# Another hand-written order for batch 0 of a hash-masked attention followed by a gated MLP

## The chip, the cores and the metric

The kernel runs on one core of one Trainium2 chip. The time is that of the device, in microseconds, from one launch of the whole program; the median of several runs counts. The profile is of one execution, whose own time is given beside the span of its instructions.

## The reference

Attention over 4 batches, 8 heads, 768 positions and 64 numbers per head. A query sees a key only if the signs of six projections of both agree. What it gives is put together into 3072 tokens of 512 numbers, which pass a GEGLU layer with a gated residual.

```python
q_bits = (np.einsum('bhsd,dk->bhsk', q, proj) > 0)
k_bits = (np.einsum('bhsd,dk->bhsk', k, proj) > 0)
mask = q_bucket[:, :, :, None] == k_bucket[:, :, None, :]
scores = np.where(mask, scale * np.matmul(q, k.transpose(0, 1, 3, 2)), -1e9)
attn = softmax(scores)
x = np.matmul(attn, v).transpose(0, 2, 1, 3).reshape(B * S, H * D)
g = x @ w_gate
ffn_out = (0.5 * g * (1 + erf(g / sqrt(2))) * (x @ w_val)) @ w_out
out = x + ffn_out / (1 + exp(-(x @ w_res)))
```

## The kernel before

**Tiling.** Two heads make a pair, four pairs a batch, so there are 16 pairs, numbered 0 to 15; pairs 0 to 3 are batch 0. Side 0 of a pair is q, side 1 is k. Positions are laid out as 128 partitions by 6 tiles for each head. An operand tile `aug` has 64 rows of data and 7 rows of hash bits, so that one product gives the score and the mask together.

**Making an operand.** `load` brings q or k into `ld` (four buffers for each side), `load_v` brings v into `ldv` (three buffers). `tr` transposes 32x32 blocks on VectorE into `t32`; `hash_mm` multiplies these with the projection on TensorE in fp32 (jobs h00 to h33, four pieces for each group of pairs in `HASHES`); `hash_tok` turns the sums back (tk); `bits` writes the signs beside the data in one of four `nat` tiles (bt). `cast` writes the data there in bf16 on GpSimd (cs). A `nat` tile is shared by a pair's side and the same side of the pair two further on. The operand is then turned either on TensorE, six tile transposes by `turn_pe` (tp, with pair, side and head in its name) and a copy out of PSUM by `turned` (td), or by one DMA transpose on SyncE's queue, `turn` (tu). For q and k of pairs 1 to 3 the first way is taken, for pairs 4 to 7 the second. `bits` of a k side in batch 0 has two of its four writes on GpSimd and two on VectorE.

**Values.** `vals_a` casts v to bf16 with a column of ones (va), `vals_s` sums v (vs), both on GpSimd.

**A score piece.** Each pair has nine pieces; batch 0 has s0 to s35. `scores` writes 1024 columns of PSUM from TensorE (two buffers, `sc_ps`) and ScalarE's exp (L553) empties them into a ring of nine places. `values` (v0 to v35) multiplies eight blocks of it with v. `finish` (fin) divides by the sum; for pairs 0 and 1 of batch 0 a DMA transpose turns the result, for pairs 2 and 3 TensorE does (`x_turn`, jobs xt2 and xt3).

**The order.** The scheduling is manual: each engine runs its instructions in the order in which the program issues them, and waits where an operand is not ready. What stands ahead of the list is fixed: the first loads (those of pair 0, then `FIRST_LOADS` in its order, all on SyncE's queue), the hashes of pair 0's first head, and on GpSimd in this order the cast of pair 1's q, `vals_a(0)`, the cast of pair 1's k, the copies that make `projw` (needed by every h job) and `vals_s(0)`. Then the jobs of `ORDER` are issued one after the other, s0 to s35 among them, ending with g0 and g1 (the first three of four products of the gate and the value of block 0), xt3 and three hash pieces. Jobs ho and hoq are the fp32 hashes of pair 0's second head, bo0 and bo1 their bits.

After it `gate_val(0)` runs twelve blocks m of the hidden layer: gate product, value product (both L566), gelu on ScalarE (L583), product on VectorE (L586). `BESIDE[m]` lists the jobs that are issued behind block m. Batches 1 to 3 run in loops: score pieces with the output products (L598, L614) of the batch before between them, then their own `gate_val`.

**Weights.** `load_w` issues the next of twelve weight loads on GpSimd's queue, whichever w job is met: w0 to w7 are gate and value by turns in quarters of three blocks each, w8 is the residual gate's matrix, w9 to w11 the output matrix in thirds.

Of the kernel before, what the change touches and what calls it, by code (L numbers as in the profile page):

```python
# [13 lines left out]
PSUM = bass.MemoryType.PSUM  # L14


FIRST_LOADS = [(1, "q"), (0, "v"), (1, "k"), (2, "q"), (2, "k"), (2, "v"), (3, "q"), (3, "k"), (1, "v")]
HASHES = [(0, (1,)), (1, (2, 3)), (2, (4, 5)), (3, (6, 7))]
X_PE = 2
ORDER = """  # L20
trq tpB tdk tdq trk s0 hoq tr10 ld50 s1 bo0 s2 ho bo1 tp001 td001 s3 tp011 td011a ld40 tr11 ld51 v0
v1 cs21 td011b s4 s5 h00 h01 h02 h03 tr20 s6 s7 v2 v3 v4 tk0 bt10 bt11 tp100 tp110 td100 td110 tr21
s8 tr30 tr31 tp111 td111 cs31 s9 tp101 td101 s10 w0 v5 v6 v7 v8 s11 cs20 s12 ld61 fin00 ld41 h10 h11
w1 s13 h12 h13 fin01 cs30 s14 lv3 ld70 s15 va1 v9 v10 v11 s16 tk1 bt20 bt21 bt31 tp200 tp210 td200
td210 vs1 s17 tp211 td211 cs41 tr50 s18 tp201 td201 va2 s19 tp310 vs2 s20 vs3 bt30 td310 v12 v13 s21
v14 fin10 s22 tp300 tr40 w2 tp301 s23 v15 tr51 s24 lv4 va4 v16 v17 s25 v18 s26 v19 v20 v21 td301
td300 s27 fin11 v22 s28 cs50 tp311 s29 ld71 v23 fin20 w3 w4 s30 lv5 w5 v24 v25 td311 s31 v26 fin21
va3 tr41 v27 s32 w6 v28 v29 v30 s33 xt2 s34 v31 s35 gelu tr61 v32 v33 v34 g0 v35 fin30 op40 g1 fin31
xt3 ld60 h20 h21 h22 w7
"""  # L30
BESIDE = [
    "vs4 lv6 cs40 h23 tk2 bt41",
    "cs51 bt50",
    "tu50 cs70 tr70",
    "bt40 tu40 cs60 w8 w9 w10 w11",
    "bt51",
    "tr71",
    "tu51",
    "tr60",
    "h30 h31 h32 tu41 cs61 h33 tk3 bt60 bt61 tu60 tu61",  # L40
    "cs71 bt71 tu71",
    "bt70 tu70",
    "pr40 rp40",
]

@with_exitstack
def kernel(
# [57 lines left out]
    def load(p, side, eng=None):  # L105
        b, hp = divmod(p, HP)
        s = ld_pool.tile([P, HT, D], FP32, tag=f"ld{side}", name=f"ld{side}")
        (eng or nc.sync).dma_start(
            s.rearrange("p (h t) d -> p h (t d)", h=2),
            (q, k)[side][b, 2 * hp:2 * hp + 2].rearrange("h (p t) d -> p h (t d)", t=T))  # L110
        raw[p, side] = s

    def load_v(p):
        b, hp = divmod(p, HP)
        vs = ldv_pool.tile([P, 2, T, D], FP32, tag="ldv", name="ldv")
        nc.sync.dma_start(
            vs, v[b, 2 * hp:2 * hp + 2].rearrange("h (p t) d -> p h t d", t=T))
        rawv[p] = vs
# [3 lines left out]
    def load_head(p, side, hi, eng):  # L122
        b, hp = divmod(p, HP)
        if (p, side) not in raw:
            raw[p, side] = ld_pool.tile([P, HT, D], FP32, tag=f"ld{side}", name=f"ld{side}")
        eng.dma_start(raw[p, side][:, hi * T:(hi + 1) * T].rearrange("p t d -> p (t d)"),
                      (q, k)[side][b, 2 * hp + hi].rearrange("(p t) d -> p (t d)", t=T))
# [6 lines left out]
    load_head(0, 1, 1, nc.sync)  # L134
    for what in FIRST_LOADS:
        load_v(what[0]) if what[1] == "v" else load(what[0], "qk".index(what[1]))
# [769 lines left out]
```

## Time and profile before

| what | us |
|---|---|
| median of 3 runs | 340.84 (340.73 to 341.19) |
| the profiled execution, its own time | 340.31 |
| its span, first to last instruction | 338.6 |
| first exp of batch 0 begins | 7.80 |
| first gate product of batch 0 begins | 44.38 |
| first product of the output stage (L598) begins | 80.37 |

A row of a timeline has the start in us from the span's beginning, the time taken, engine, line, operation, output and inputs, shape, and how many neighbouring instructions of one kind it holds; in brackets stands the idle time of the engine before it and what ended that. PE is TensorE, ACT ScalarE, DVE VectorE, POOL GpSimd; PEld is TensorE's loading of weights, which runs beside its products. SPq is SyncE's queue, where a row's duration is that of the issue.

### The profile page before, as it was taken

The page shows a single profiled execution, that of the slowest core. Times are in us where ns is not written, and L with a number is a line of the kernel's source. Part 1 is how long each engine was busy: PE and PEld are TensorE (multiplying, and loading weights), DVE is VectorE, ACT ScalarE, POOL GpSimd, SP SyncE. Part 2 cuts the span into 40 slices and gives each one's busy share as a digit, 9 for nine tenths or more (in the row PEclk, how much of TensorE's full clock was granted, in tenths as well). Part 3 has the DMA queues.
Part 4 walks back from the last instruction along what each step waited for, and adds up shares of the span by engine and source line. Part 5 has one row for each costly group of instructions (what it writes and reads, how often), then busy time and mean ns, then how long its engine had stood idle before and what let it go on. Part 6 is the DMA issues. An engine that isn't in the chain of part 4 may idle for free.

```text
span 338.6 us, 7598 instructions
## 1 busy us (share of the span) xinstructions
PE 333.2 (98%) x3058; PEld 203.1 (60%) x3058; DVE 216.9 (64%) x418; ACT 206.2 (61%) x232; POOL 171.9 (51%) x220
## 2 busy tenths in 40 slices
PE   8999999999999999999999999999999999999995
PEld 4667766655666655655666665656566665666444
DVE  6889457574445748888887766887897444343343
ACT  4889963317999952235999982233999984223220
POOL 5879920410665306998999704998998000000000
PEclk9999999999999999999999999999999999999999
DMA  7997897799876634350488832551261420000012
GB/s 211 379 249 169 160 252 128 132 190 199 240 164 187 207 94 99 73 96 0 126 219 204 277 106 62 102 96 28 48 148 39 97 56 33 31 0 2 31 64 94
DMA packets 71459, 43.09 MB, mean 127 GB/s; under 512 B 49536, under 2 KB 68480, under 8 KB 71424
## 3 DMA queue, kind: packets, MB, share of 16 engines
q1 hardware_dynamic: 65008, 37.37, 43.7%
q0 software_dynamic: 6336, 5.24, 10.1%
q8 instruction: 24, 0.39, 0.5%
q14 instruction: 11, 0.09, 0.1%
q10 hardware_dynamic: 80, 0.00, 0.0%
HBM read 29.56 MB, written 6.29 MB: 106 GB/s over the span
## 4 chain that ended last, share of the span: by engine, by line
PE 91%; ACT 4%; DVE 3%; issue 1%; DVEq 0%; ACTq 0%
PE sp L566 35%; PE fps L614 18%; PE sp L542 17%; PE av L515 9%; PE rps L598 6%; ACT hh L553 4%; PE hs L283 2%; DVE hh L586 1%; PE wps L189 1%; PE pt L384 1%; PE hs L330 1%; DVE nat L319 1%; DVE hsum L361 0%; PE pt L499 0%; DVE o L621 0%
## 5 line engine op out<-in xcount | busy, mean ns | idle before, releaser
L553 ACT ACTIVATE e<-sp 128x1024 bf16<-128x1024 f32 x108 | 109.0, 1028 | 8.1 <-PE sp L542 2.8
L357 POOL TENSOR_TENSOR pd<-ld,prow 128x768 f32<-128x768 f32 x48 | 86.1, 1811 | 36.8 <-PE hs L283 32.6
L583 ACT ACTIVATE gt<-sp 128x768 bf16<-128x768 f32 x48 | 38.9, 810 | 89.8 <-PE sp L566 89.8
L542 PE MATMUL sp<-aug,aug 71*128 71x256 bf16 (+1 forms) x384 | 85.5, 325 | 0.1
L614 PE MATMUL fps<-wo,hh 128*128 128x512 bf16 (+2 forms) x312 | 79.5, 362 | 0.0
L566 PE MATMUL sp<-x_sb,wv 128*128 128x512 bf16 (+1 forms) x384 | 70.9, 326 | 0.4 <-DVE hh L586 0.4
L566 PE MATMUL sp<-x_sb,wg 128*128 128x512 bf16 (+1 forms) x384 | 70.9, 326 | 0.1
L586 DVE TENSOR_TENSOR hh<-gt,sp 128x768 bf16<-128x768 bf16 x48 | 45.8, 954 | 39.0 <-PE sp L566 34.2
L515 PEld LDWEIGHTS <-e 128*128 128x128 bf16 x864 | 40.2, 97 | 25.1
L566 PEld LDWEIGHTS <-wv 128*128 128x128 bf16 x384 | 37.6, 98 | 25.5 <-issue 0.8
L566 PEld LDWEIGHTS <-wg 128*128 128x128 bf16 x384 | 36.9, 98 | 25.8 <-issue 1.7
L361 DVE TENSOR_REDUCE hsum<-pd 128x12 f32<-128x768 f32 x48 | 44.4, 943 | 0.5
L515 PE MATMUL av<-va,e 128*128 128x65 bf16 x864 | 43.4, 193 | 0.0
L614 PEld LDWEIGHTS <-hh 128*128 128x128 bf16 x312 | 28.1, 97 | 21.8
L553 ACT ACTIVATE hh<-sp 128x1024 bf16<-128x1024 f32 x36 | 34.5, 1024 | 3.4 <-PE sp L542 3.0
L542 PEld LDWEIGHTS <-aug 71*128 71x128 bf16 x384 | 29.5, 97 | 11.0 <-issue 1.1
L617 DVE SCALAR_TENSOR_TENSOR fps<-th,fps 128x512 f32<-128x512 f32 (+2 forms) x26 | 16.9, 650 | 28.3 <-PE fps L614 27.8
L598 PE MATMUL rps<-wr,x_sb 128*128 128x512 bf16 x96 | 27.1, 379 | 0.0
L494 DVE COPY av<-av 128x390 f32<-128x390 f32 x24 | 13.7, 571 | 19.6 <-PE av L490 19.6
L602 ACT ACTIVATE th<-rps 128x512 f32<-128x512 f32 x24 | 14.3, 594 | 18.5 <-PE rps L598 18.5
L223 POOL TENSOR_SCALAR nat<-ld 128x768 bf16<-128x768 f32 (+1 forms) x16 | 13.0, 813 | 18.6 <-DMA aug<-nat 18.0
L265 DVE STREAM_TRANSPOSE t<-ld 128x768 f32<-128x768 f32 (+1 forms) x24 | 21.9, 925 | 0.1
(77 smaller groups left out, 259.6 us busy)
## 6 DMA issues: line engine op xcount, KB each, us to landing
ldv<-in_v_dram SPq DMA_DIRECT2D x16, 384.0 KB, 5.1
out_dram<-o SPq DMA_DIRECT2D x23, 256.0 KB, 2.0
ld<-in_q_dram SPq DMA_DIRECT2D x15, 384.0 KB, 5.6
ld<-in_k_dram SPq DMA_DIRECT2D x15, 384.0 KB, 6.0
wg<-in_moe_w_gate_dram POOLq DMA_DIRECT2D x4, 384.0 KB, 9.1
wv<-in_moe_w_val_dram POOLq DMA_DIRECT2D x4, 384.0 KB, 11.8
wo<-in_moe_w_out_dram POOLq DMA_DIRECT2D x3, 512.0 KB, 11.8
wr<-in_moe_w_res_dram POOLq DMA_DIRECT2D x1, 512.0 KB, 7.7
```

Of the source, the lines that this page charges most:

```text
L265: nc.vector.transpose(t32[p, side][:, sl].rearrange("p c h n -> p (c h n)"), raw[p, side][:, sl].rearrange("p c d -> p (c d)"))
L357: nc.gpsimd.tensor_mul(pd, raw[x], prow[:, j].unsqueeze(1).to_broadcast([P, HT, D]))
L361: nc.vector.tensor_reduce(stripes(hsum6)[:, :, :, j], hparts.pop((x, j)).rearrange("p (a c) d -> p a c d", a=3), axis=mybir.AxisListType.X ...
L515: nc.tensor.matmul(av[p, hi][:, qt, :], e[:, off:off + P], va[:, hi, jt, 0:D + 1], start=first, stop=(p >= HP and jt == T - 1), skip_group ...
L542: nc.tensor.matmul(sp[:, off:off + nq * P], ks[0:KA, hi * T + jt, :], qs[0:KA, hi * T + qt0:hi * T + qt0 + nq, :], start=True, stop=True)
L553: nc.scalar.activation(e, sp, AF.Exp, scale=float(ALPHA))
L566: nc.tensor.matmul(sp[:, c0:c1], w[:, kk, bass.ts(m, P)], xs[:, kk, c0:c1], start=(kk == 0), stop=(kk == KM - 1))
L583: nc.scalar.activation(gt, sp[:, 0:S], AF.Gelu)
L586: nc.vector.tensor_mul(hidden[b][:, m, :], gt, ps[1][:, 0:S])
L598: nc.tensor.matmul(rps, x_sb[b][:, kk, t, :], wr[:, kk, :], start=(kk == 0), stop=(kk == KM - 1))
L614: nc.tensor.matmul(fps[:, cs], hh[:, m, bass.ts(t, P)], wo[:, m, cs], start=(m == 0), stop=(m == KF - 1))
L617: nc.vector.scalar_tensor_tensor(fps[:, cs], th[:, cs], 1.0, fps[:, cs], op0=ALU.add, op1=ALU.mult)
```

## The change

Three lists are replaced; no function is touched and the jobs are the same. `FIRST_LOADS` has the v loads of pairs 0 and 1 further ahead and pair 3's q and k last. `ORDER` puts the same jobs in another order, and some jobs move between it and `BESIDE`: cs40, cs51, vs4, lv6 and tr60 are now in `ORDER`, w7 and ld71 in `BESIDE`.

```diff
-FIRST_LOADS = [(1, "q"), (0, "v"), (1, "k"), (2, "q"), (2, "k"), (2, "v"), (3, "q"), (3, "k"), (1, "v")]
+FIRST_LOADS = [(0, "v"), (1, "q"), (1, "k"), (2, "q"), (2, "k"), (2, "v"), (1, "v"), (3, "q"), (3, "k")]
 ORDER = """
-trq tpB tdk tdq trk s0 hoq tr10 ld50 s1 bo0 s2 ho bo1 tp001 td001 s3 tp011 td011a ld40 tr11 ld51 v0
-v1 cs21 td011b s4 s5 h00 h01 h02 h03 tr20 s6 s7 v2 v3 v4 tk0 bt10 bt11 tp100 tp110 td100 td110 tr21
-s8 tr30 tr31 tp111 td111 cs31 s9 tp101 td101 s10 w0 v5 v6 v7 v8 s11 cs20 s12 ld61 fin00 ld41 h10 h11
-w1 s13 h12 h13 fin01 cs30 s14 lv3 ld70 s15 va1 v9 v10 v11 s16 tk1 bt20 bt21 bt31 tp200 tp210 td200
-td210 vs1 s17 tp211 td211 cs41 tr50 s18 tp201 td201 va2 s19 tp310 vs2 s20 vs3 bt30 td310 v12 v13 s21
-v14 fin10 s22 tp300 tr40 w2 tp301 s23 v15 tr51 s24 lv4 va4 v16 v17 s25 v18 s26 v19 v20 v21 td301
-td300 s27 fin11 v22 s28 cs50 tp311 s29 ld71 v23 fin20 w3 w4 s30 lv5 w5 v24 v25 td311 s31 v26 fin21
-va3 tr41 v27 s32 w6 v28 v29 v30 s33 xt2 s34 v31 s35 gelu tr61 v32 v33 v34 g0 v35 fin30 op40 g1 fin31
-xt3 ld60 h20 h21 h22 w7
+trq tpB tdq s0 tdk trk hoq bo0 ho bo1 s1 tr10 tr11 lv3 s2 tp011 td011a tp001 v0 td001 v1 s3 td011b
+cs21 h00 h01 s4 tr20 s5 ld40 h02 h03 s6 v2 v3 v4 cs20 s7 tr21 tk0 bt10 bt11 tp100 tp110 td100 td110
+ld50 s8 ld51 fin00 tp111 tr30 ld41 s9 tp101 td101 vs2 s10 tr31 v5 v6 v7 v8 fin01 s11 td111 s12 h10
+va2 h11 h12 h13 s13 s14 va1 v9 v10 v11 v12 s15 tk1 bt20 bt21 tp210 td210 vs1 cs30 s16 tp200 td200
+ld60 w0 w1 w2 va3 bt30 s17 v13 v14 vs3 tr40 s18 tp211 cs41 td211 s19 v15 v16 s20 fin10 tp201 lv4 s21
+bt31 cs31 va4 v17 v18 td201 s22 tp301 td301 s23 ld61 tp300 td300 s24 tp310 tr50 fin11 cs40 v19 ld70
+s25 v20 v21 vs4 lv5 s26 td310 s27 v22 tr61 s28 tr41 v23 v24 v25 s29 tp311 td311 cs51 fin20 s30 v26
+cs50 s31 v27 tr51 s32 w3 v28 v29 v30 s33 fin21 xt2 s34 lv6 v31 v32 fin30 op40 s35 v33 v34 g0 gelu
+v35 fin31 w4 w5 w6 g1 xt3 h20 h21 h22 tr60
 """
 BESIDE = [
-    "vs4 lv6 cs40 h23 tk2 bt41",
-    "cs51 bt50",
-    "tu50 cs70 tr70",
-    "bt40 tu40 cs60 w8 w9 w10 w11",
-    "bt51",
-    "tr71",
-    "tu51",
-    "tr60",
-    "h30 h31 h32 tu41 cs61 h33 tk3 bt60 bt61 tu60 tu61",
-    "cs71 bt71 tu71",
-    "bt70 tu70",
-    "pr40 rp40",
+    "h23 tk2 bt41",
+    "bt50 tu50",
+    "bt40 tu40 cs60",
+    "bt51 w7",
+    "pr40 rp40 tu41 cs61",
+    "tr70",
+    "ld71 tr71 w8 w9 w10",
+    "",
+    "",
+    "tu51 cs71 h30 h31 h32 h33 tk3 bt60 bt61 tu61 cs70",
+    "bt70 tu70 bt71",
+    "w11 tu60 tu71",
 ]
```

## The prediction

> **What bounds the kernel now.** I read the page's totals, ScalarE's timeline of batch 0, the chain of waits, then GpSimd's and SyncE's timelines.
>
> ```profile
> PE 333.2 (98%) x3058; PEld 203.1 (60%) x3058; DVE 216.9 (64%) x418; ACT 206.2 (61%) x232; POOL 171.9 (51%) x220
> ...
> 7.80 4.15 ACT L553 ACTIVATE hh<-sp 128x1024 bf16<-128x1024 f32 x4 [0.68 <-PE sp L542]
> 12.39 1.94 ACT L553 ACTIVATE hh<-sp 128x1024 bf16<-128x1024 f32 x2 [0.44 <-PE sp L542]
> 14.79 1.94 ACT L553 ACTIVATE hh<-sp 128x1024 bf16<-128x1024 f32 x2 [0.46 <-PE sp L542]
> 17.46 2.85 ACT L553 ACTIVATE hh<-sp 128x1024 bf16<-128x1024 f32 x3 [0.73 <-PE sp L542]
> 20.80 2.86 ACT L553 ACTIVATE hh<-sp 128x1024 bf16<-128x1024 f32 x3 [0.49 <-PE sp L542]
> 23.90 21.09 ACT L553 ACTIVATE hh<-sp 128x1024 bf16<-128x1024 f32 x22 [0.24 <-PE sp L542]
> ```
>
> PE looks full over the whole span, but in batch 0 its busy time counts overlapping products. These rows show who sets the pace there: 36 exps from 7.80 to 44.99, the last 22 (exp14 to exp35) in 21.09, or 0.95 from one to the next. Before exp14 ACT waited five times for a score, 2.4 together.
>
> ```profile
> 38.85 0.49 PE av L515 x16
> 39.34 0.44 PE sp L542 x3
> ...
> 40.02 0.17 PE av L487
> ...
> 45.52 0.24 PE av L515 x8
> ...
> 49.76 20.96 PE sp L566 x128
> ```
>
> Behind the last exp the chain goes on with v35 (45.52), division, xt3, the fourth gate product and gelu, and from 49.76 PE sets the end alone: 128 products in 20.96, so 1.31 for a group of eight and 2.62 for a block. So a delay of exp35 moves everything behind it, and a better batch 0 wins hardly more than the 2.4. From the first two rows: a score holds PE for 0.44, a values job for 0.245, and 0.17 more where it closes a head (L487).
>
> **The start, up to exp14.** I walk through the new list engine by engine, with these rows.
>
> ```profile
> 7.17 0.59 PE L542 MATMUL sp<-aug,aug 71*128 71x512 bf16 x2
> 7.60 0.84 PE L330 MATMUL hs<-t,projs 128*128 128x192 f32 x4
> 8.28 1.19 PE L542 MATMUL sp<-aug,aug 71*128 71x256 bf16 x6
> ...
> 7.84 1.42 DVE L265 STREAM_TRANSPOSE t<-ld 128x384 f32<-128x384 f32 x2
> ...
> L265 DVE STREAM_TRANSPOSE t<-ld 128x384 f32<-128x384 f32 x2 | 1.1, 558 | 0.0
> ...
> 3.14 0.47 SPq L116 DMA_DIRECT2D ldv<-in_v_dram  x1
> ...
> ldv<-in_v_dram SPq DMA_DIRECT2D x1, 384.0 KB, 6.2
> ...
> 8.74 0.83 POOL L223 TENSOR_SCALAR nat<-ld 128x768 bf16<-128x768 f32 x1
> ...
> 10.27 0.15 POOL L433 MEMSET va<- 128x12 bf16 x1
> ...
> 11.18 0.87 POOL L183 COPY projw<-projn 32x12 f32<-32x12 f32 x4
> ...
> 12.79 1.43 PE hs L283 x16
> ...
> 22.47 0.79 PE hs L283 x16
> ```
>
> s0 needs nothing that moves: PE at 7.17, exp0 at 7.80, so an exp begins 0.64 behind its score, and exp0, one of four in 4.15, ends at 8.82. Now hoq and ho both stand before s1. ho needs trk: 7.84 + 0.56 = 8.40, then 0.12 to TensorE (an estimate; GpSimd takes 0.16 behind VectorE in the tk1 rows below), then 0.68 for its products (7.60 to 8.28): s1 at 9.20, exp1 at 9.84, **1.02 idle**. exp2 follows at 10.79.
>
> v0 and v1 now stand before s3, and v0 needs `va0`. GpSimd first casts pair 1's q, whose load is now second in the list; what was second landed at 3.14 + 6.2 = 9.34, so the cast starts 0.60 later than its 8.74, `va0` ends at 11.02 and `projw` at 12.65. v0 at 11.12, s3 at 11.61, exp3 at 12.25: **0.44**. h00 and h01 stand before s4 and need `projw`: 12.77 and half of 1.43 give s4 at 13.50, exp4 at 14.14: **0.87**. exp5 and exp6 follow at 15.09 and 16.04 without a wait, where the undivided hash cost 0.46; s6 stands behind h02 and h03 and gets its buffer when exp4 ends, at 15.2.
>
> v2, v3 and v4 with the close of a head (0.91) stand ahead of s7: 16.55, exp7 at 17.19, **0.13** behind the end of exp6. tk0 starts when h03 is through, 15.3, and with VectorE's six bit writes (0.6 + 1.4, by the tk1 rows below) it is 17.4 when tp110, which stands before s8, can begin. Six transposes take 0.33, s8 is at 17.86, exp8 at 18.50: **0.29** where it was 0.73. exp9 and exp10 follow at 19.45 and 20.40. v5 to v8 with a close (1.15) between s10 and s11 put exp11 at 21.79: **0.37** for 0.49. h10 to h13 now all stand between s12 and s13, begin at 22.0 and take 1.5 (twice 0.79, less the overlap in the middle): s13 at 23.50, exp13 at 24.14, **0.38**. exp14 comes at 25.09 instead of 23.90. The start loses **1.2**: seven waits, 3.5 together, for five with 2.4 (a wait also ends the overlap of two exps, 0.07 each). Bounds: nothing lost, if each new wait hides in the next, and 2.0, if the three that hang on GpSimd and ho are each 0.3 longer.
>
> **GpSimd's queue from tk1 to cs31.** This is the larger term. cs31, the cast of pair 3's k, now stands behind tk1 and a long queue on GpSimd; tp310, which reads it, stands on PE right behind s24, ahead of v19 and s25.
>
> ```profile
> 23.40 0.58 DVE L303 STREAM_TRANSPOSE ht<-hs 128x384 f32<-128x384 f32 x1 [0.81 <-PE hs L283]
> 24.02 1.88 DVE L319 TENSOR_SCALAR nat<-ht 32x72 bf16<-32x72 f32 x8
> ...
> 24.14 2.06 POOL L319 TENSOR_SCALAR nat<-ht 32x72 bf16<-32x72 f32 x4 [1.15 <-DVE ht L303]
> 26.28 0.99 POOL L440 TENSOR_TENSOR v<-ldv 128x384 f32<-128x384 f32 x1
> ...
> 28.32 0.83 POOL L225 CAST nat<-ld 128x768 bf16<-128x768 f32 x1
> 29.09 0.83 POOL L432 CAST va<-ldv 128x768 bf16<-128x768 f32 x1
> ...
> 29.92 1.00 POOL L440 TENSOR_TENSOR v<-ldv 128x384 f32<-128x384 f32 x1
> ...
> L208 POOL DMA_DIRECT2D wg<-in_moe_w_gate_dram x4 | 3.4, 838 | 0.0
> ...
> L208 POOL DMA_DIRECT2D wv<-in_moe_w_val_dram x4 | 3.1, 785 | 0.0
> ```
>
> From start to start these give 2.14 for four bit writes, 2.04 for a vs, 0.77 for a cast, 0.83 for a va, 0.84 and 0.79 for a weight issue. Behind tk1 GpSimd now has half of bt21 1.07, vs1 2.04, cs30 0.77, w0 to w2 2.46, va3 0.83, vs3 2.04, cs41 0.77, half of bt31 1.07, cs31 0.83: 11.9. By the walk h13 ends at 23.7, tk1 at 24.3; GpSimd starts 0.16 later (23.98 to 24.14 in the rows), cs31 ends at 36.3, and tp310 can start at 36.4.
>
> PE is there earlier: exp24 is due at 25.09 + 10 x 0.95 = 34.6 and s24 has left PE at 34.2. PE waits 2.2, and behind it stand tp310 (six products, 0.33), v19 (0.245) and s25: exp25 at 37.65, due 35.54: **2.1 lost**. Nothing later in the list has an operand that late, so exp35 ends at 37.65 + 9.5 + 1.0 = 48.2. The jobs between there and the gate keep their order and move along. Before the change the same four bit writes lay ahead of vs1 and cs31 ahead of s9, so nobody waited. With weight issues at nothing the queue is 9.4, and no wait is left; with a quarter more on each it is 12.5, and 2.7 are lost. I take the rows' means, since they are of these very instructions.
>
> [...]
>
> **Behind the exps** I take nothing. The transposes and weights:
>
> ```profile
> aug<-nat SPq DMA_TRANSPOSE x3, 3.7
> ...
> aug<-nat SPq DMA_TRANSPOSE x4, 6.5
> ...
> 63.61 0.83 POOL L223 TENSOR_SCALAR nat<-ld 128x768 bf16<-128x768 f32 x1 [4.38 <-DMA aug<-nat]
> ...
> wv<-in_moe_w_val_dram POOLq DMA_DIRECT2D x1, 384.0 KB, 7.0
> ...
> wv<-in_moe_w_val_dram POOLq DMA_DIRECT2D x3, 384.0 KB, 13.8
> ...
> 65.63 0.95 DVE L586 TENSOR_TENSOR hh<-gt,sp 128x768 bf16<-128x768 bf16 x1 [0.76 <-PE sp L566]
> 68.23 0.95 DVE L586 TENSOR_TENSOR hh<-gt,sp 128x768 bf16<-128x768 bf16 x1 [1.65 <-PE sp L566]
> ```
>
> Between 54 and 63 three transposes took 3.7; from 63.5 on, beside wr and wo, four took 6.5. The new list spares some of them that, but those who waited are casts on GpSimd, which no product waits for: worth nothing. The thing made later is w7, behind cs60 on GpSimd. bt40 stands one block earlier, so cs60 goes from 63.61 to about 61.0 and w7 to 61.8 (before the shift of 3.2, which moves both sides); block 9's value product needs it at 49.76 + 8 x 2.62 + 1.31 = 72.0. That leaves 10.2: enough for 7.0, and 3.6 too little for 13.8, which was with six weights queued together. tr71 now stands on VectorE between the products of blocks 6 and 7, the two L586 rows, and needs ld71, which SyncE issues behind tu40 and tu41. tu40 lands at about 61.0 by what was said of cs60, and was issued 3.7 earlier; if ld71 goes out by then and takes 6.2, as the load above, it lands at 67.2 at the latest. The transpose takes about twice the 0.56 of half its size, so it is due at 68.23 - 1.1 = 67.1. I take it as just in time, at nothing. Each us later would be lost.
>
> **Sum.** 340.31 for the profiled execution, plus 1.2, plus 2.1: 343.5, with the rounding of the walk (48.2 - 44.99 = 3.2). The median of the runs lies 0.53 above that execution: **344.0**. The terms' bounds give 342.6 to 345.2 about it.
>
> **Rivals.** GpSimd in time: the list's own spans on POOL are called rough; if the queue is 2.2 shorter, only the start's loss stays: 342.0. Against it: the rows follow each other without a gap, so their starts are a good measure.
>
> Faster: the divided hash brings tk0 and tk1 forward. Its place is exp5 to exp14, its price the last four waits of before, 0.46 + 0.73 + 0.49 + 0.24 = 1.9, so 338.9. It decides only if tk1 ends by 34.2 - 0.16 - 11.9 = 22.1, nearly 2 before its 23.98; ho and `projw`, which my walk has as late, would have to hide.
>
> No change: half of that is won and GpSimd's wait gives it back, 340.8.
>
> w7 late by 3.6 on top of the forecast: 347.6; ld71 late by one would be less. [...]
>
> The change does what it says, but that is in the forecast at nothing.
>
> **How the numbers follow.** Forecast 0.65, GpSimd in time 0.12, faster 0.10, no change 0.06, w7 late 0.04, held issues 0.03. The range 341.5 to 345.7 leaves out the faster and the unchanged case and w7, 0.20. Faster by over 0.2% (0.7 us, about what a measurement here can tell) 0.10, within it 0.06, slower 0.84.
>
> **What would show it.** In ACT's timeline a wait of about 1 before exp1, one near 0.9 before exp4, and one near 2 before exp25 put down to a PE that waits for a cast on GpSimd, with the gate's long run of products 3 later. The forecast is wrong if exp25 follows exp24 closely, if exp14 starts before 23.9, or if PE stands between blocks of the gate.

## The result and the profile after

| kernel | median us | lowest to highest | runs |
|---|---|---|---|
| before | 341.03 | 340.73 to 341.63 | 6 |
| after | 349.98 | 347.70 to 350.32 | 6 |

The ratio is 1.0252, 95% interval 1.0224 to 1.028: slower, as forecast, but by 8.95 us and not by 3.2. The profiled execution took 350.32, with a span of 348.6.

The page of the kernel after: span, busy times, two rows of the slices, and the shares of the chain that ended last.

```profile
span 348.6 us, 7598 instructions
...
PE 337.9 (97%) x3058; PEld 206.2 (59%) x3058; DVE 217.0 (62%) x418; ACT 206.5 (59%) x232; POOL 171.8 (49%) x220
...
PE   8999499999999999999999999999999999999995
...
PEclk9999679999999999999999999999999999999999
...
PE 91%; DVE 3%; POOL 3%; issue 2%; ACT 0%; DVEq 0%; POOLq 0%
```

The counts are the same (3058 products, 418, 232, 220). TensorE's busy time is 4.7 longer for the same products, one slice, 34.9 to 43.6, has a 4, and in it and the next one the granted clock (PEclk, the share of its full speed that TensorE was given, in tenths) falls to 6 and 7. ScalarE's timeline of batch 0 shows where:

```profile
8.82 1.02 ACT L553 ACTIVATE hh<-sp 128x1024 bf16<-128x1024 f32 x1 [0.93 <-PE sp L542]
10.99 1.94 ACT L553 ACTIVATE hh<-sp 128x1024 bf16<-128x1024 f32 x2 [1.15 <-PE sp L542]
13.13 1.02 ACT L553 ACTIVATE hh<-sp 128x1024 bf16<-128x1024 f32 x1 [0.19 <-PE sp L542]
14.44 2.85 ACT L553 ACTIVATE hh<-sp 128x1024 bf16<-128x1024 f32 x3 [0.29 <-PE sp L542]
17.52 1.02 ACT L553 ACTIVATE hh<-sp 128x1024 bf16<-128x1024 f32 x1 [0.23 <-PE sp L542]
18.85 2.85 ACT L553 ACTIVATE hh<-sp 128x1024 bf16<-128x1024 f32 x3 [0.30 <-PE sp L542]
22.20 1.94 ACT L553 ACTIVATE hh<-sp 128x1024 bf16<-128x1024 f32 x2 [0.49 <-PE sp L542]
24.61 11.33 ACT L553 ACTIVATE hh<-sp 128x1024 bf16<-128x1024 f32 x12 [0.47 <-PE sp L542]
41.98 1.02 ACT L553 ACTIVATE hh<-sp 128x1024 bf16<-128x1024 f32 x1 [6.04 <-PE sp L542]
43.72 1.94 ACT L553 ACTIVATE hh<-sp 128x1024 bf16<-128x1024 f32 x2 [0.71 <-PE sp L542]
46.19 1.02 ACT L553 ACTIVATE hh<-sp 128x1024 bf16<-128x1024 f32 x1 [0.53 <-PE sp L542]
48.14 6.74 ACT L553 ACTIVATE hh<-sp 128x1024 bf16<-128x1024 f32 x7 [0.92 <-PE sp L542]
```

The last exp ends at 48.14 + 6.74 = 54.88; before it was 23.90 + 21.09 = 44.99. These 9.89 have three parts. The first exp is 1.02 later (8.82 for 7.80). Ahead of s0 only tdk, trk and the first v load changed places, and the same list gave 7.66 in another run, so this part comes back below as a matter of chance. Up to exp14 the new order adds 0.63: it begins one exp behind 24.61, at 25.55, so 16.73 behind the first exp, and 16.10 before. The rest, 8.24, lies between exp14 and exp35: a wait of 6.04 before exp25, and behind it three more, 0.71 + 0.53 + 0.92, where there was none.

The chain of waits of the kernel after leads through GpSimd to that first wait (start, duration, what):

```profile
24.11 0.59 DVE ht L303
24.86 0.46 POOL nat L319
...
28.02 0.79 POOL nat L223
28.82 2.71 issue
31.52 0.98 POOL wg L208
32.51 0.75 POOL wv L208
33.26 0.74 POOL wg L208
33.99 0.83 POOL va L432
...
38.86 0.84 POOL nat L225
39.74 0.85 PE pt L384 x6
```

That is the queue of the forecast job by job: tk1 (L303), bits (L319), vs1, cs30 (28.02), w0, w1, w2, va3, vs3, cs41, bits, and cs31 at 38.86, which releases tp310. One row was not in it: ahead of w0 GpSimd stood still for 2.71, "issue", waiting for nothing that the profile shows.

The windows view of the kernel after, cut at steps of 3.41 us (columns: length, busy time of PE, PEld, DVE, ACT and POOL with their instructions, granted clock, DMA share, GB/s), shows the second thing that was not in it:

```profile
30.61:34.02 3.41, 3.41 (x46) 2.69 (x45) 2.11 (x5) 3.41 (x5) 2.49 (x4) 1.00 0.30 12
34.02:37.44 3.42, 0.67 (x4) 0.10 (x1) 2.17 (x4) 1.92 (x3) 3.26 (x7) 1.00 1.22 183
37.44:40.85 3.41, 1.11 (x15) 1.11 (x16) 0.22 (x1) 0.00 (x0) 3.17 (x7) 0.50 1.30 222
40.85:44.26 3.41, 3.41 (x28) 2.07 (x26) 2.08 (x3) 1.57 (x2) 2.36 (x5) 0.50 1.01 336
44.26:47.67 3.41, 3.41 (x39) 2.55 (x38) 0.00 (x0) 2.42 (x3) 0.00 (x0) 0.50 0.00 0
47.67:51.09 3.42, 3.41 (x52) 2.48 (x51) 2.60 (x6) 2.95 (x4) 2.64 (x4) 1.00 0.03 7
```

TensorE was busy for 0.67 us of the 3.42 that begin at 34.02, and from the next one on its clock is exactly half, for three windows, 10.24 us, although in the last two of them it had work all the time. At full clock a window does 46 or 52 products, at half 28 and 39. That is where the waits of 0.71, 0.53 and 0.92 are from. The clock before was full from 4.56 on.

Behind the exps nothing moved. TensorE's timeline of the kernel after:

```profile
59.62 1.46 PE L566 MATMUL sp<-x_sb,wg 128*128 128x512 bf16 x8
...
90.23 1.03 PE L598 MATMUL rps<-wr,x_sb 128*128 128x512 bf16 x4
```

The gate's long run begins at 59.62 for 49.76, the first output product at 90.23 for 80.37: 9.86 both times, the delay of exp35.

### The profile page after: what moved, and what is told of

Same layout as the page of the kernel before. It is cut to its first block, busy times and chain, and to the rows that moved or that the text cites. A ratio compares the mean times of both kernels' runs of the same rounds, so it can differ in the third digit from the quotient of the medians.

```text
span 348.6 us, 7598 instructions
## 1 busy us (share of the span) xinstructions
PE 337.9 (97%) x3058; PEld 206.2 (59%) x3058; DVE 217.0 (62%) x418; ACT 206.5 (59%) x232; POOL 171.8 (49%) x220
## 4 chain that ended last, share of the span: by engine, by line
PE 91%; DVE 3%; POOL 3%; issue 2%; ACT 0%; DVEq 0%; POOLq 0%
PE sp L566 34%; PE fps L614 18%; PE sp L542 17%; PE av L515 10%; PE rps L598 6%; PE hs L283 2%; DVE hh L586 1%; PE hs L330 1%; PE pt L384 1%; PE wps L189 1%; POOL v L440 1%; DVE nat L319 1%; POOL nat L319 1%; POOL wg L208 0%; POOL nat L225 0%
## 5 line engine op out<-in xcount | busy, mean ns | idle before, releaser
L542 PE MATMUL sp<-aug,aug 71*128 71x256 bf16 (+1 forms) x384 | 87.3, 331 | 0.1
```

The costliest lines, as they stand in the source:

```text
L542: nc.tensor.matmul(sp[:, off:off + nq * P], ks[0:KA, hi * T + jt, :], qs[0:KA, hi * T + qt0:hi * T + qt0 + nq, :], start=True, stop=True)
```

## The experiments

Theory from this profile: one cast, cs31, comes too late, and this costs twice, as a stand of TensorE and as the halved clock that follows it. Rivals: the start is the main loss; or the issues of weights on GpSimd are. In the diffs, jobs alone on a line are those of `ORDER`.

**cs31 early.** The changed kernel with the pair's last bits and cast ahead of the weight issues.

```diff
-... tp210 td210 vs1 cs30 s16 tp200 td200
+... tp210 td210 vs1 cs30 bt31 cs31 s16 tp200 td200
...
-bt31 cs31 va4 v17 v18 ...
+va4 v17 v18 ...
```

> The changed kernel with bt31 and cs31 directly behind cs30, ahead of w0 to w2, va3, vs3 and cs41 on GpSimd; nothing else. Theory (the stall is GpSimd's queue in front of cs31, and the halved clock only follows from PE's idle stretch): tp310 does not wait, the granted clock stays 1.00 through batch 0, exp14 to exp35 run without a gap, exp35 ends some 1.5 behind the 44.99 of before; time 341.6 to 342.8. Rival A (only the queue's position moves: what held GpSimd 2.7 ahead of w0 still delays a later operand): still over 343. Rival B (the clock is halved by something else, such as the weights' transfers): a half-clock stretch near 37 to 48 stays, and the time is over 344.

Measured: 341.24, ratio to before 1.0011 (1.0 to 1.0022); clock 1.0 over the whole span. ScalarE's and GpSimd's timelines of this kernel:

```profile
23.93 21.86 ACT L553 ACTIVATE hh<-sp 128x1024 bf16<-128x1024 f32 x23 [0.47 <-PE sp L542]
...
30.42 0.98 POOL L208 DMA_DIRECT2D wg<-in_moe_w_gate_dram  x1 [0.34 <-issue]
```

The last 23 exps run without a gap. Of the 8.95, all but 0.23 (0 to 0.75) hang on the place of these two jobs, and the whole of the new start costs no more than that remainder. The time is a little under the 341.6 to 342.8 expected: exp35 ends 0.80 behind the 44.99 of before, and not 1.5.

**Weights behind cs31.** The other way to bring cs31 forward.

```diff
-ld60 w0 w1 w2 va3 bt30 ...
+ld60 va3 bt30 ...
...
-bt31 cs31 va4 v17 v18 ...
+bt31 cs31 w0 w1 w2 va4 v17 v18 ...
```

> The changed kernel with w0, w1 and w2 moved behind cs31, so that no weight is issued on GpSimd between tk1 and cs31. If the 2.71 that GpSimd stood still ahead of w0 belong to the first weight issue: cs31 ends near 39.7 - 2.7 - 2.5 = 34.5, PE waits less than 0.5 for it, the wait of 2.7 shows up ahead of w0 again, behind cs31, and the time is 342 to 343. If they belong to that moment (something else held GpSimd from 28.8 to 31.5): va3 waits in w0's place, cs31 ends near 37.2, PE waits 2.5, and the time is 344 to 347.

Measured: 341.7, ratio 1.0017 (1.0001 to 1.0034); exps from 24.01 without a gap. GpSimd's timeline of this kernel:

```profile
28.16 0.82 POOL L432 CAST va<-ldv 128x768 bf16<-128x768 f32 x1
...
33.77 0.98 POOL L208 DMA_DIRECT2D wg<-in_moe_w_gate_dram  x1
```

Neither row has a wait. The stand-still went neither with w0 nor to va3, which took w0's place. Neither case of the expectation had this, and the time lies under both.

**Filler products.** The changed kernel with 24 products of 512 columns into an unused place of PSUM, issued ahead of tp310, so that TensorE works instead of standing.

```diff
-... s24 tp310 tr50 ...
+... s24 warm tp310 tr50 ...
...
+    def warm():
+        junk = mm_ps.tile([P, 512], FP32, tag=take(), name="junk")
+        for _ in range(24):
+            nc.tensor.matmul(junk, ones(P), ones(512), start=True, stop=True)
```

> The changed kernel with 24 products of 512 columns (5.1 us at full clock, written to a PSUM buffer that nobody reads) on PE just ahead of tp310, so that PE is busy while it would have waited for cs31. GpSimd's queue is untouched. Theory (the idle wait costs twice: itself, and a clock at half speed afterwards): cs31 still ends near 39.7, tp310 begins there, but the granted clock stays 1.00, exp25 begins near 41.0 instead of 41.98 and exp25 to exp35 need 9.5 instead of 11.9; time about 3.4 below the changed kernel, 346 to 347. Rival (the slow stretch behind the wait comes from something else): no better than the changed kernel, 349 to 350.

Measured: 346.63 (346.22 to 346.92), ratio 1.0173 (1.0155 to 1.0191), clock 1.0. TensorE's and ScalarE's timelines of this kernel:

```profile
33.83 5.41 PE L766 MATMUL junk<-const-bfloat16-1.0 128*128 128x512 bf16 x24
39.08 0.49 PE L384 MATMUL pt<-ident,nat 128*71 128x128 bf16 x6
...
40.35 10.60 ACT L553 ACTIVATE hh<-sp 128x1024 bf16<-128x1024 f32 x11 [5.18 <-PE sp L542]
```

cs31 is as late as it was, and exp25 still waits 5.18, but behind it the eleven exps run without a gap. So the halved clock alone cost 349.98 - 346.63 = 3.35, and the stand alone 346.63 - 341.24 = 5.4. The border between the two is not sharp: the filler held TensorE until 39.08, 0.4 past the start that the cast's end at 38.61 allowed, so the clock's part may be up to 0.4 more and the stand's as much less. Counted from the first exp of each profile, the last exp ends 2.8 earlier here than in the changed kernel, and 5.7 later than with cs31 early.

**ho ahead of s1, in the kernel before.** One part of the new start alone.

```diff
-trq tpB tdk tdq trk s0 hoq tr10 ld50 s1 bo0 s2 ho bo1 tp001 td001 ...
+trq tpB tdk tdq trk s0 hoq bo0 ho bo1 tr10 ld50 s1 s2 tp001 td001 ...
```

> The kernel before with one part of the new start: both fp32 hashes and their bits (hoq bo0 ho bo1) ahead of s1. Theory: exp1 waits about 1.0 for s1, because ho waits for trk; the earlier bits give some of it back at tp001 and tp011, so that exp14 comes 0.3 to 0.9 later than 23.90 and the time is 341.3 to 342.0. Rival (the wait at exp1 is hidden by later waits that shrink): exp14 at 23.9 and no change, 340.6 to 341.2.

Measured: 341.64, ratio 1.0021 (1.0005 to 1.0038), with a wait of 1.08 before exp1 and exp14 0.62 later, counted from the first exp. This term is real and had about the size worked out for its wait. In the changed kernel exp14 comes 16.73 behind the first exp, here 16.72, so its other moves up to exp14 came to nothing together.

**w0 alone moved up.** To see whether the stand-still of 2.71 belongs to the first weight issue or to the place in GpSimd's list.

```diff
-... tp101 td101 vs2 s10 tr31 ...
+... tp101 td101 vs2 s10 w0 tr31 ...
...
-ld60 w0 w1 w2 va3 ...
+ld60 w1 w2 va3 ...
```

> The changed kernel with w0 alone moved up behind s10; w1 and w2 stay behind ld60. In the changed kernel GpSimd stood still 2.71 ahead of w0 (28.82), and PE then waited 4.99 for cs31. Theory A, the stand-still belongs to this place of GpSimd's list: it comes now ahead of w1, and cs31 ends only the issue's 0.98 earlier, PE waits 4.0, TensorE's clock still falls to half, about 349.0. Theory B, it belongs to w0, the first weight issue: it comes at s10, where GpSimd has time, cs31 ends 0.98 + 2.71 = 3.7 earlier, PE waits 1.3, the clock stays full, and the time is 349.98 - 3.7 - 3.4 = 342.9 (3.4 is what the halved clock cost by the run with the filler products). Rival, it falls by chance with the time: no wait at either place and 342.9 as well, with no row of GpSimd showing it.

Measured: 345.37 (344.18 to 345.78), ratio 1.013 (1.0111 to 1.0149). No issue waited, neither w0 at 19.00 nor w1 at 27.88: of the stand-still that was the rival's case, and neither theory's. TensorE stood 1.38, about as theory B and the rival had it, but the clock was halved all the same, which I had left out for so short a stand. Rows of TensorE's timeline and of the windows of this kernel:

```profile
35.23 0.83 PE L384 MATMUL pt<-ident,nat 128*71 128x128 bf16 x6 [1.38 <-POOL nat L225]
```

```profile
31.88:35.30 3.42, 1.98 (x19) 1.19 (x18) 2.58 (x5) 3.15 (x4) 3.13 (x7) 1.00 0.95 146
35.30:38.71 3.41, 3.41 (x36) 2.65 (x37) 2.44 (x4) 1.02 (x1) 3.25 (x6) 0.50 0.49 81
38.71:42.12 3.41, 3.08 (x50) 2.39 (x49) 0.00 (x0) 2.98 (x4) 0.14 (x2) 1.00 0.91 319
```

A window in which TensorE was busy for 1.98 of 3.42 is followed by one at half clock.

**vs3 behind cs31.** The stand made 2.04 shorter.

```diff
-... s17 v13 v14 vs3 tr40 ...
+... s17 v13 v14 tr40 ...
...
-bt31 cs31 va4 ...
+bt31 cs31 vs3 va4 ...
```

> The changed kernel with vs3 (two sums on GpSimd, 2.04) moved from ahead of cs31 to behind it; w0, w1, w2 stay. PE's wait ahead of tp310 should shrink from 4.99 to about 3.0. It tells from what idle time on TensorE's clock is halved. Theory A, any wait of 3 halves it as the 4.99 did (its record went to half 2.7 after PE's last product): the stretch stays and only the 2.04 are won, about 347.9. Theory B, an idle time of 3.0 is too short: the clock stays full and the time is 349.98 - 2.04 - 3.4 = 344.5, which is my blind forecast's 344.0 with a wait of its size. If GpSimd's stand-still ahead of w0 fails to come, 2.7 less in either case.

Measured: 347.22 (345.51 to 348.92), ratio 1.019 (1.0156 to 1.0224). TensorE stood 3.26 (the stand-still ahead of w0 was 3.03 here) and its clock was halved, as theory A had it, but not always as long: the four runs took 345.51, 346.14, 348.92 and 348.29 at mean clocks of 0.995, 0.990, 0.985 and 0.985. A loss of 0.005 of the clock over 344 us is 344 x 0.005 / 0.5 = 3.4 us at half, one window.

**w0, w1, w2 behind vs3.** The same work ahead of cs31 in another order.

```diff
-ld60 w0 w1 w2 va3 bt30 s17 v13 v14 vs3 tr40 ...
+ld60 va3 bt30 s17 v13 v14 vs3 w0 w1 w2 tr40 ...
```

> The changed kernel with w0, w1, w2 moved behind va3 and vs3, still ahead of cs41, bt31 and cs31: GpSimd's queue from tk1 to cs31 holds the same work in another order. Theory A, the stand-still of 2.7 has a fixed end (in five profiles w0 began 1.4 to 1.5 behind the end of the same 8 KB packet on the instruction queue, at 30.4 to 31.5): w0 comes at about 30.5 to 31.5 here and waits 0 to 0.5, cs31 ends 2.2 to 2.7 earlier, PE stands 2.2 to 2.8, the length that my forecast had; the clock is halved for one or two stretches of 3.4 as with a stand of 1.38 and 3.26, and the time is 345.4 to 347.5. Theory B, GpSimd stands still wherever the first weight issue stands behind vs1: the wait stays 2.7 and the time is 350. If the length alone counted, as I forecast, 344 to 345.

Measured: 347.09 (345.61 to 347.54), ratio 1.0165 (1.0127 to 1.0203). GpSimd's and TensorE's timelines of this kernel:

```profile
30.83 0.10 POOL L444 MEMSET vsum<- 128x2 bf16 x1
30.98 0.98 POOL L208 DMA_DIRECT2D wg<-in_moe_w_gate_dram  x1
...
36.32 0.85 PE L384 MATMUL pt<-ident,nat 128*71 128x128 bf16 x6 [2.33 <-POOL nat L225]
```

w0 follows vs3 with 0.05 between them, TensorE stands 2.33. This is the queue as my forecast summed it, with the stand that it gave (2.2), and yet the time is 3 above the forecast: the halved clock alone, for one to three windows in the four runs.

**cs31 late in the kernel before.** Whether the cast is enough, without the rest of the change.

```diff
-... tp111 td111 cs31 s9 ...
+... tp111 td111 s9 ...
...
-... va2 s19 tp310 vs2 s20 ...
+... va2 s19 vs2 cs31 tp310 s20 ...
```

> The kernel before with one job moved: cs31 from ahead of s9 to behind vs2, right ahead of tp310, so that the cast ends at about 32.8 on GpSimd and PE, which is there at about 31.4, stands for 1.4; nothing else of the change. Theory, the wait at tp310 is what makes the changed kernel slow, and its price is more than its length: a stand of 1.4 halves TensorE's clock for a stretch as it did with w0 moved up (PE stood 1.38 there, 345.37), and the time is 343 to 345. Rival, a stand of 1.4 costs its length less ScalarE's lead of two scores at most: 341.0 to 342.4, clock full.

Measured: 348.95 (347.27 to 349.53), ratio 1.0221 (1.0199 to 1.0243). I had misjudged when TensorE gets there: it is done with what stands ahead at 28.76, not 31.4. TensorE's and ScalarE's timelines of this kernel:

```profile
33.16 0.86 PE L384 MATMUL pt<-ident,nat 128*71 128x128 bf16 x6 [4.39 <-POOL nat L225]
...
34.97 1.02 ACT L553 ACTIVATE hh<-sp 128x1024 bf16<-128x1024 f32 x1 [4.99 <-PE sp L542]
37.02 1.02 ACT L553 ACTIVATE hh<-sp 128x1024 bf16<-128x1024 f32 x1 [1.03 <-PE sp L542]
```

So it could not tell what a stand of 1.4 costs. What it does show: with the old start, the old weights and one cast moved, the time is only 1.03 us under the changed kernel's. The stand is 4.39, the half clock 6.83, two windows.

**The start as before, on top of cs31 early.** Pair 1's q first among the loads, s1 ahead of ho, v0 and v1 behind s3, s4 and s5 ahead of h00.

```diff
-FIRST_LOADS = [(0, "v"), (1, "q"), ...
+FIRST_LOADS = [(1, "q"), (0, "v"), ...
...
-trq tpB tdq s0 tdk trk hoq bo0 ho bo1 s1 tr10 tr11 lv3 s2 tp011 td011a tp001 v0 td001 v1 s3 td011b
-cs21 h00 h01 s4 tr20 s5 ld40 h02 h03 s6 v2 v3 v4 cs20 s7 tr21 tk0 ...
+trq tpB tdk tdq trk s0 hoq tr10 s1 bo0 s2 ho bo1 tp001 td001 s3 tp011 td011a lv3 tr11 v0
+v1 cs21 td011b s4 s5 h00 h01 h02 h03 tr20 s6 s7 ld40 v2 v3 v4 cs20 tr21 tk0 ...
```

> The version with bt31 and cs31 directly behind cs30 (341.24, no wait at tp310, exp14 at 23.93 with a first exp at 8.20), and on top of it the start of the list as it was before the change: pair 1's q first among the further loads, s1 ahead of ho, tr11 later, v0 and v1 behind s3, s4 and s5 ahead of h00. It tells how much of the time the new start costs. My prediction's walk (start loses 1.2): 341.24 - 1.2 = 340.0. What the changed kernel's profile gave (0.6 once the later first exp is taken off): 340.6. Rival, the start costs nothing in the end: 341.2. exp14 should begin 16.1 behind the first exp (before: 23.90 - 7.80) if the start is undone fully, against 16.7 in the changed kernel and 15.7 in the version without the stall.

Measured: 341.27, ratio 1.0015 (1.0005 to 1.0025), nothing won over 341.24. The waits before exp1 and exp3 are gone, but one of 1.43 stands before exp8, where tk0 now comes behind the undivided hash and behind tr21 on VectorE; exp13 begins 16.12 behind the first exp, against 15.73 in the run without it (the 23.93 and the 15.7 of the expectation were exp13's, not exp14's). So this run doesn't price the new start by itself, and it doesn't tell which of the two holds tk0 back.

**Two tries for a version that beats both.** The kernel before with the hash divided (its diff is shown), and the run above with the hash divided and tk0, the bits and the first turns ahead of cs20 and tr21.

```diff
-s4 s5 h00 h01 h02 h03 tr20 s6 s7 v2 v3 v4 tk0 ...
+s4 h00 h01 s5 h02 h03 tr20 s6 s7 v2 v3 v4 tk0 ...
```

> The kernel before with one thing of the change: pair 1's hash divided in two, h00 h01 behind s4 and h02 h03 behind s5 (before: all four behind s5). Theory (my rival 'faster', made smaller by what the changed kernel showed): s5 comes with the first half's 0.72 ahead of it instead of none, s6 with the other half, so exp6's wait of 0.46 becomes 0.2 to 0.3, tk0 is earlier and exp8's 0.73 becomes 0.3 to 0.5; exp14 at 15.4 to 15.7 behind the first exp instead of 16.1 and the time 340.3 to 340.6. Rival, the same work stands ahead of s8 in any order and the sum of the waits stays 2.4: 341.0.

> The version of the last batch with the start put back (341.27, waits of 0.44, 0.46, 1.43, 0.49, 0.47 before the exps), with the hash divided as in the run beside it and with tk0 and the bits ahead of cs20 and tr21 as in the kernel before. If the wait of 1.43 came from tr21 standing ahead of tk0 on VectorE, it goes to 0.3 to 0.7 and the time to 340.2 to 340.6, a little under the kernel before. Rival, the order behind s8 asks for it: 341.2.

Measured: 341.27, ratio 1.0009 (1.0 to 1.0019), and 341.97, ratio 1.0024 (1.0014 to 1.0034). In the first, exp6's wait of 0.46 became two, 0.69 and 0.29, and exp8's 0.73 stayed; in the second, exp8's 1.43 went to 0.73 and exp13's rose from 0.47 to 0.90. Both miss: the sum of the waits did not fall. None of the versions beats the kernel before.

## Why the forecast was right in direction and wrong in size

| term | forecast | measured | by |
|---|---|---|---|
| start, up to exp14 | 1.2 | 0.2 to 0.6 | cs31 early; the profile after |
| TensorE's stand at tp310 | 2.2 (2.1 lost) | 4.99 (5.4 lost) | profile after; filler products |
| pace behind the stand | 0 | 3.35 | filler products |
| behind the exps | 0 | 0 | 9.86 at both ends of the gate |

**The start.** The waits came at the places named: exp1 1.15 (forecast 1.02), exp3 0.19 (0.44), exp4 0.29 (0.87), exp7 0.23 (0.13), exp8 0.30 (0.29), exp11 0.49 (0.37), exp13 0.47 (0.38). The step that was off is exp4's. In this execution the scores began 1.02 late and the copies on GpSimd that make `projw` only 0.44 (11.62 for 11.18), so more of their delay was hidden; with an early first exp, at 7.66 and 7.71, the runs with vs3 behind cs31 and with the filler had 0.54 and 0.70 there. And not all of a late exp14 reached the end: with cs31 early it came 0.57 later than before, counted from the first exp, and the end of exp35 0.40.

**GpSimd's queue.** The sum of 11.9 from bits to cs31 was right for the work: 14.83 measured (24.86 to 39.69), less 2.71, is 12.1. What failed is the step from rows of work to a finishing time: the queue also held a stand-still that no row of the kernel before showed. In the run with the weights behind vs3, where it does not come, TensorE stood 2.33 for my 2.2.

**The stand's price.** This is the step that failed most. I took "PE waits 2.2" at "2.1 lost" and let exp25 to exp35 follow at 0.95. In no run with a stand of 1.38 or more did they: the granted clock was at half when TensorE came back, or went there 0.07 (w0 moved up) and 1.12 us later (vs3 moved: back at 37.03, half from 38.15). The queue's bounds (0 to 2.7 lost) missed the 5.4, and nothing in any bound stood for the slow pace behind it; the granted clock, the row that could have shown it, is full all through the kernel before from 4.56 on, where TensorE's longest wait in the profile is 0.8. The 342.6 to 345.2 of the sum do not follow from the terms' bounds either: 0 to 2.0 and 0 to 2.7 give 340.8 to 345.5.

**Behind the exps** holds: w7 was issued at 71.60 and landed 6.7 later, at 78.3, where block 9's value product came at 59.62 + 8 x 2.62 + 1.31 = 81.9. That fewer transposes lie beside the weights is worth nothing here, as said. The forecast also had a chance of 0.03 for held issues, and the upper end of its range, 345.7, stood for weight issues lengthened by VectorE's copies. No run shows that: in the kernel after, the three issues among VectorE's operand copies (L393) took 0.98, 0.75 and 0.75, 2.48 for the 2.46 of the sum.

**The rivals** fall: GpSimd was not in time; tk1 ended at 24.7 and not by 22.1, and the divided hash alone wins nothing (341.27), so "faster" and "no change" had no ground.

## What to carry to other kernels

Where one product waits for a late operand, price it as the wait plus what TensorE does at half clock behind it: here stands of 1.4 to 5 us cost their length and 2.7 to 3.8 more. When jobs are moved, follow the operand that ends up last in the slowest queue (here a cast on GpSimd) to the product that stands first in line for it, and put the weight issues behind it, not ahead. If a stand cannot be avoided, products on junk data in it can be tried: here they kept the clock at 1.0 and, with the cast as late as it was, brought 3.35 us back.

## What the runs showed of the hardware

**In these traces the clock fell and came back in steps of 3.41 us.** The half stretches are 3.41 (w0 moved up, vs3 moved), 6.83 (the late cast in the kernel before) and 10.24 (after, weights behind vs3), so one, two or three windows. TensorE's busy share of the window ahead of the first half one was 0.20 (after), 0.58 (w0 moved up), 0.33 (vs3 moved), 0 (the late cast) and 0.50 (weights behind vs3); windows at full clock with 0.70 (vs3 moved, one window earlier) and 0.80 (after, from 6.71 to 10.13) were followed by full clock; at half clock 0.79 (the late cast) and 0.80 (weights behind vs3) were followed by another half window. How many windows follow differs from run to run of one kernel: the changed kernel's 347.70 has a mean clock of 0.990, the other five 0.985. A stand of 1.38, less than a window, was enough (w0 moved up), and the changed kernel got full clock back only after two windows in which TensorE was busy throughout (3.41 of 3.41 in each). Whether a share decides, and which, and why one such window was enough with w0 moved up and not in the changed kernel, stays open.

**A stand-still ahead of a weight issue.** In six profiles w0 came behind vs1 on GpSimd's queue, at around 30 us:

| kernel | w0 begins | GpSimd stood |
|---|---|---|
| after | 31.52 | 2.71 |
| cs31 early | 30.42 | 0.34 |
| filler products | 30.45 | 2.41 |
| start as before | 30.64 | 0.68 |
| vs3 behind cs31 | 30.86 | 3.03 |
| weights behind vs3 | 30.98 | 0.05 |

By this table, how long GpSimd stood goes by when it was ready: that lies between 27.83 and 30.93, w0's start between 30.42 and 31.52. In the kernel after, an 8 KB packet on an instruction queue (q14) ends at 29.98, 1.54 before w0; in five profiles, by the expectation of the run with the weights behind vs3, w0 began 1.4 to 1.5 behind the end of that packet. No run takes the packet away, so whether w0 waits for it is not shown. With w0 moved up to 19.00, or to 33.77 behind cs31, it did not wait; nor is it known why w1 in the same place (27.88) did not. VectorE works without a gap from 28.16 to 32.26 in the changed kernel; but with the weights behind cs31, where the list has the same VectorE jobs, va3 and vs3 ran on GpSimd from 28.16 on without a wait.

**The first exp comes by chance.** It begins between 7.66 and 8.82 in the seven profiles with the new list ahead of it, between 7.68 and 8.60 in the six with the old one. Of the two profiles of before and after, the one with the later first exp also has the later start of the granted clock's record: 4.56 with 7.80 (before), 6.71 with 8.82 (after), both at full. Differences in the start of two profiles are read from the first exp on.
